# A Fourier mixing layer before a softmax MLP: the step back of the transform on half-size matmul tiles, with the halves joined on VectorE

## Chip, cores and metric

The kernel runs on one core of a Trainium2 chip. The metric is the time of one execution on the device, in microseconds. The kernel before takes 1681.73 us (median of 3 runs, 1681.02 to 1687.88).

## What is computed

Two blocks in sequence, all in float32. First, along the 3136 positions of each of 8 sequences and for each of 256 channels, a real Fourier transform, a product with a complex filter, and the transform back. Then, for each of the 25088 tokens, a layer with 1024 hidden values, their softmax used as a gate, a normalization, and a projection back to 256 values.

```python
X = np.fft.rfft(x, axis=1)                       # x: (8, 3136, 256)
y = np.fft.irfft(X * (filt_r + 1j * filt_i), n=3136, axis=1)
x = y.reshape(25088, 256)
h = x @ w_in                                     # 256 -> 1024
e = np.exp(h - h.max(-1, keepdims=True))
solu = h * e / (e.sum(-1, keepdims=True) + 1e-9)
ln = (solu - solu.mean(-1)) / np.sqrt(solu.var(-1) + 1e-6) * g_ln
return ln @ w_out                                # 1024 -> 256
```

## The kernel before

The transform of length 3136 = 49 x 64 is done in three parts. The **first step** is a transform over 49 (products `pa`). The **spectrum** is a transform over 64, forward (`pb`), the product with the filter on VectorE, and inverse (`pc`). The **step back** over 49 (`py`) writes the sequence into the buffer `y`, channels on the partitions, from which the hidden layer takes its tokens. Intermediate rows go through DRAM. The step back of a sequence is eight pieces; a piece loads 100 rows of 4 KB and makes 4 of the 32 mirrored column pairs:

```python
    def fetch_back(e, ch, rows_pool, split=None):
        split = split or whole
        if rows_pool is not None:
            t4s[e, ch] = rows_pool.tile([P, NCH, C], FP32, ..., tag="r")[0:NK]
        split((nc.sync.dma_start if split is by_16 else nc.gpsimd.dma_start, nc.sync.dma_start),
              t4s[e, ch], d2[e].rearrange("s (a n) c -> (s a) n c", a=4)[:, NCH*ch:NCH*ch+NCH, :])

    def back(e, ch, cb, evac):                   # cb: half of the channels
        ps = ps_t.tile([P, 512], FP32, name=f"py_{e}_{ch}_{cb}", tag="t")
        psv = ps[:, 0:NCH * NR].rearrange("p (m r) -> p m r", r=N1)
        for i in range(NCH):                     # 100 rows deep, 128 wide, 98 columns
            nc.tensor.matmul(out=psv[:, i:2*NCH-i:2*NCH-1-2*i, :],
                             lhsT=t4s[e, ch][:, i, cb*P:cb*P+P], rhs=wi_t, start=True, stop=True)
        ...
        evac(out=y[:, cb, t0:t0+S].rearrange("p (r m j) -> p m j r", ...)[...],
             in_=psv.rearrange("p (m j) r -> p m j r", m=2))
```

Both matrix products of the MLP use Strassen's scheme, seven products of half size where eight would be needed, on **pairs** of token tiles: 256 tokens, 98 pairs in all. `product(j, m)` is one of the seven hidden products of pair j (512 columns each; m in 1, 2, 6, 7, 5, 3, 4 is their order in time), `project(p, m)` one of the seven of the projection (four matmuls of 128 columns each; order 5, 3, 4 in the even step, 1, 2, 6, 7 in the odd one), which belongs to a pair of some steps before. What several products share is kept by a copy on ScalarE (`keep`, `keep_out`) and completed on VectorE (`finish`, `finish_out`):

```python
    def product(j, m):
        bank = {1: 0, 6: 0, 5: 0, 3: 0, 2: 1, 7: 2, 4: 2}[m]
        if m in (1, 2, 7):
            ms[j, bank] = (ps_t.tile(..., tag="t") if m == 2 else ps_m.tile(..., tag=f"m{bank}"))
        ...
        nc.tensor.matmul(out=ms[j, bank], lhsT=lhsT, rhs=w_in_sb[:, w, :],
                         start=m in (1, 2, 7), stop=True, skip_group_check=True)

    def finish_out(p, i, n, kept, bank):
        ot, rs = out_half(p, i, n)
        if kept is None:
            nc.vector.tensor_scalar(out=ot, in0=pos[p, bank], scalar1=rs, ..., op0=ALU.mult)       # L809
        else:
            nc.vector.scalar_tensor_tensor(out=ot, in0=pos[p, bank], scalar=rs,                    # L811
                                           in1=out_half(p, *kept)[0], op0=ALU.mult, op1=ALU.add)
```

The program is a list of steps, two for a pair, and its order on each engine is the order of the text. `early` and `late` hold the transform's jobs of a step: the two halves of a piece of the step back (`cb` 0 early, 1 late), the spectrum's forward products (early), its first multiplication (late) and, in the following odd step, its second multiplication and its inverse products. The parts that matter here, shortened:

```python
    def step(k):
        j, odd = divmod(k, 2)
        ...
        for job in stores[k]: job()                       # odd: difference() of the first step, on VectorE
        if not odd:
            product(j, 1); keep(j, k, 0)
            project(p, 5); keep_out(p, 1, (0, 1))
            product(j, 2)
        else:
            product(j, 5); keep(j, k - 1, 1)
        turn(k - 3)                                       # 32x32 transposes on VectorE
        if not odd:
            finish_out(p, 1, 1, (0, 1), 1); finish(j, k, 0, (k, 0), 1)
        else:
            finish(j, k, 1, (k - 1, 1), 2)
        for job in products[k]: job()                     # second multiplication of the spectrum
        exponential(k - 2)
        for job in early[k]: job()
        if not odd:
            product(j, 6); keep(j, k + 1, 0)
            project(p, 3); project(p, 4)
            ...
            product(j, 7)
        else:
            project(p, 1); keep_out(p, 0, (0, 0)); project(p, 2); finish_out(p, 0, 0, (0, 0), 1)
            product(j, 3); product(j, 4)
            ...
            project(p, 6); project(p, 7)
        normalize(k - 2)
        if not odd:
            finish_out(p, 0, 1, None, 0); finish_out(p, 1, 0, (1, 0), 1); store_out(p)
        else:
            finish(j, k - 1, 1, None, 0); finish(j, k, 0, (k, 0), 2)
            keep_out(p, 1, (1, 0))
        for job in late[k] + loads[k]: job()
```

Which steps hold which jobs is a fixed table. For the sequences 2 to 7 the pieces of the step back stand in even steps, spectrum units start in even steps, and pieces of the first step stand in odd ones; a pair may hold one of each, two of them, one or none. The PSUM pools are `ps_t` (two banks), `ps_b` (two, spectrum), `ps_m` (two, hidden) and `ps_o` (two, projection).

Of the kernel before, what the change touches and what calls it, by code (L numbers as in the profile page):

```python
# [17 lines left out]
P = 128  # L18
# [31 lines left out]
def dft_tables():  # L50
# [19 lines left out]
    for a, part, sign in ((0, 0, 1), (1, 1, -1), (2, 1, 1), (3, 0, 1)):  # L70
# [16 lines left out]
    wq[:, :N1, :, :NK // 2] = wf[1].reshape(N1, NS, 2, 2).transpose(0, 3, 1, 2).reshape(N1, 2, NK // 2)  # L87
    return wf.reshape(NR, NK).astype(f32), wq.reshape(P, 2, 64).astype(f32), \
        wi.reshape(NK, NR).astype(f32), de.astype(f32)
# [3 lines left out]
def kernel(  # L93
# [11 lines left out]
    wf_host, wq_host, wi_host, de_host = dft_tables()  # L105
    wf_dram = nc.inline_tensor(wf_host, name="wf_tbl").ap()
    wq_dram = nc.inline_tensor(wq_host, name="wq_tbl").ap()
    wi_dram = nc.inline_tensor(wi_host, name="wi_tbl").ap()
    de_dram = nc.inline_tensor(de_host, name="de_tbl").ap()
# [16 lines left out]
    wi_t = consts.tile([NK, NR], FP32, name="wi_t")  # L126

# [210 lines left out]
    def fetch_back(e, ch, rows_pool, split=None):  # L338

        split = split or whole  # L340
        if rows_pool is not None:
            t4s[e, ch] = rows_pool.tile([P, NCH, C], FP32, name=f"t4_{e}_{ch}", tag="r")[0:NK]
        split(
            (nc.sync.dma_start if split is by_16 else nc.gpsimd.dma_start, nc.sync.dma_start), t4s[e, ch],
            d2[e].rearrange("s (a n) c -> (s a) n c", a=4)[:, NCH * ch:NCH * ch + NCH, :])
# [14 lines left out]
    with ExitStack() as st:  # L360
# [163 lines left out]
        for i in range(units):  # L524
# [8 lines left out]
            if i == 0:  # L533
                nc.gpsimd.dma_start(out=wi_t, in_=wi_dram)
                nc.gpsimd.dma_start(out=wq_t, in_=wq_dram)
                nc.gpsimd.dma_start(out=g_sb, in_=moe_g_ln.rearrange("(k p) -> p k", p=P))
            elif i != 2:
                begin({1: 2, 3: 3, 4: 4, 5: 5, 6: 6}[i])
# [4 lines left out]
        for ch in range(pieces):  # L543
            fetch_back(0, ch, None, by_16)
# [126 lines left out]
    def product(j, m):  # L671

        bank = {1: 0, 6: 0, 5: 0, 3: 0, 2: 1, 7: 2, 4: 2}[m]
        if m in (1, 2, 7):
            ms[j, bank] = (ps_t.tile([P, DFF // 2], FP32, name=f"m{m}_{j}", tag="t") if m == 2 else
                           ps_m.tile([P, DFF // 2], FP32, name=f"m{m}_{j}", tag=f"m{bank}"))
# [129 lines left out]
    def finish_out(p, i, n, kept, bank):  # L806
        ot, rs = out_half(p, i, n)
        if kept is None:
            nc.vector.tensor_scalar(out=ot, in0=pos[p, bank], scalar1=rs, scalar2=None, op0=ALU.mult)  # L809
        else:  # L810
            nc.vector.scalar_tensor_tensor(out=ot, in0=pos[p, bank], scalar=rs,  # L811
                                           in1=out_half(p, *kept)[0], op0=ALU.mult, op1=ALU.add)
# [204 lines left out]
```

## Time and profile before

| what | value |
|---|---|
| time | 1681.73 us |
| span of the profiled execution | 1680.2 us |
| mean granted clock of TensorE | 0.988 |
| HBM read and written | 124.83 MB and 81.50 MB |
| mean rate of the DMA engines | 186 GB/s |
| loads of the step back, `t<-d` by GpSimd | 56 of 400.0 KB, 4.9 us to landing |

The profile's page is one execution on the chip. A line of its groups reads: source line, engine, operation, output<-inputs by the program's names, shapes, count, then the busy time of the group, the mean of one in ns, and the idle time of the engine just before, with what ended it. PE is TensorE's matmul, PEld its weight load, DVE is VectorE, ACT ScalarE, POOL GpSimd. A float32 matmul appears as two passes, so 512 matmuls of `py` count as 1024. Matmuls are pipelined, and the end of one is modelled: the distance between two starts says what one really costs. A line of the timeline has the start in us, the length in us, then the same names and the count of instructions that are merged; a bracket gives idle time and what ended it. Source lines meant here: L353 is the matmul of the step back and L356 its copy, L680 the hidden products, L792 the projection's, L260 and L292 the first step's and the spectrum's, L313 to L315 the multiplication with the filter, L245 the difference of the first step, L738 `turn`, L704 and L701 `finish`, L723 to L728 `normalize`, L809 and L811 `finish_out`.

### The profile page before, as it was taken

Reading aid. Unit: us, or ns where it says so; the run is one execution under the profiler, and the core shown is the slowest. Engines: PE = TensorE matmul, PEld = TensorE weight load, DVE = VectorE, ACT = ScalarE, POOL = GpSimd, SP = SyncE. Lnnn points to the kernel's source line nnn. Section 1 sums busy time; section 2 is a strip of 40 time slices with the busy share of each in tenths; the row PEclk is TensorE's granted clock in tenths of the full one; section 3 lists DMA queues with packets and bytes.
Section 4 is the critical chain, followed back from the end, with each engine's and each line's share of the span. In section 5 each row is a group of like instructions: output and inputs, shape, how many; then the busy total and the mean of one; then the engine's idle time right before and its main releaser. Section 6 shows DMA issues by size and latency. Waiting matters only on the chain.

```text
span 1680.2 us, 31072 instructions
## 1 busy us (share of the span) xinstructions
PE 1597.7 (95%) x10022; PEld 1094.7 (65%) x10022; DVE 1260.4 (75%) x2619; ACT 939.3 (56%) x1730; POOL 1120.8 (67%) x1268
## 2 busy tenths in 40 slices
PE   5798899999999999999999999999999999999996
PEld 1353356766766676667766676667776777777776
DVE  1676887788777877886878777887778767787773
ACT  2154455656655565566655656556565566655551
POOL 4444786577676766697577866687576766676674
PEclk8999999999999999999999999999999999999999
DMA  9886868786787668865786667766775444444443
GB/s 264 254 278 202 255 180 243 196 220 182 191 224 222 178 182 236 228 182 150 210 243 195 176 166 220 229 181 161 204 213 161 117 125 123 103 106 105 109 112 95
DMA packets 375957, 311.72 MB, mean 186 GB/s; under 512 B 61514, under 2 KB 341571, under 8 KB 375795
## 3 DMA queue, kind: packets, MB, share of 16 engines
q1 hardware_dynamic: 306260, 169.81, 38.5%
q0 software_dynamic: 32640, 101.65, 20.5%
q10 hardware_dynamic: 36896, 38.28, 8.2%
q8 instruction: 81, 1.33, 0.3%
q14 instruction: 80, 0.66, 0.1%
HBM read 124.83 MB, written 81.50 MB: 123 GB/s over the span
## 4 chain that ended last, share of the span: by engine, by line
PE 64%; DMA 17%; DVE 8%; POOL 3%; issue 3%; SPq 2%; ACT 1%; ACTq 0%; DVEq 0%; POOLq 0%
PE m L680 26%; PE o L792 25%; DMA solu_t<-turn 7%; PE py L353 5%; DMA x<-in_x_dram 2%; DMA t<-d 2%; PE pa L260 2%; PE pb L292 2%; PE pc L292 2%; SPq L750 2%; DVE h L728 2%; DVE turn L738 1%; DMA out_dram<-ot 1%; PE pa L217 1%; DVE diff L245 1%
## 5 line engine op out<-in xcount | busy, mean ns | idle before, releaser
L730 ACT ACTIVATE e<-h,nmu 128x1024 f32<-128x1024 f32 x196 | 225.3, 1149 | 360.3 <-DVE h L728 358.8
L792 PEld LDWEIGHTS o<-w_out_sb,solu_t 128*128 128x128 f32 x3136 | 380.3, 192 | 57.8 <-issue 40.7
L792 PE MATMUL o<-w_out_sb,solu_t 128*128 128x128 f32 x3136 | 400.5, 276 | 9.1 <-DVE rsum L723 6.3
L680 PE MATMUL m<-w_in_sb,s 128*128 128x512 f32 x784 | 401.8, 604 | 4.6 <-ACT h L690 2.5
L792 PEld LDWEIGHTS o<-w_out_sb,u 128*128 128x128 f32 x2352 | 305.2, 191 | 147.4 <-issue 113.8
L658 POOL TENSOR_TENSOR u<-solu_t 128x512 f32<-128x512 f32 x98 | 145.3, 1483 | 311.0 <-DMA solu_t<-turn 179.0
L680 PE MATMUL m<-w_in_sb,y 128*128 128x512 f32 x588 | 313.8, 617 | 15.9 <-DVE nmax L704 12.8
L792 PE MATMUL o<-w_out_sb,u 128*128 128x128 f32 x2352 | 312.3, 276 | 7.0 <-ACT ot L804 6.3
L728 DVE SCALAR_TENSOR_TENSOR h<-e,rsum,h 128x1024 f32<-128x1024 f32 x196 | 289.1, 1475 | 6.9
L811 DVE SCALAR_TENSOR_TENSOR ot<-o,rs_t,ot 128x128 f32<-128x128 f32 x294 | 102.5, 349 | 206.6 <-ACT ot L804 170.3
L690 ACT COPY h<-m 128x512 f32<-128x512 f32 x294 | 173.5, 590 | 130.8 <-PE m L680 116.2
L738 DVE STREAM_TRANSPOSE turn<-h 128x1024 f32<-128x1024 f32 x196 | 242.3, 1236 | 0.8
L712 ACT ACTIVATE e<-h,nmax 128x1024 f32<-128x1024 f32 x196 | 226.1, 1154 | 0.0
L658 POOL TENSOR_TENSOR u<-solu_t,u 128x512 f32<-128x512 f32 x98 | 142.7, 1456 | 87.2 <-PE o L792 83.3
L704 DVE CUSTOM_DVE_ANT_0 h<-m,h 128x512 f32<-128x512 f32 x196 | 133.2, 679 | 82.2 <-ACT h L690 59.3
L680 PEld LDWEIGHTS m<-w_in_sb,y 128*128 128x128 f32 x588 | 95.1, 192 | 124.5 <-DVE nmax L704 67.9
L356 ACT COPY y<-py 128x392 f32<-128x392 f32 x128 | 109.6, 856 | 105.4 <-PE py L353 103.8
L353 PEld LDWEIGHTS py<-wi_t,t 100*128 100x128 f32 x1024 | 132.3, 192 | 53.9 <-issue 40.4
L680 PEld LDWEIGHTS m<-w_in_sb,s 128*128 128x128 f32 x784 | 124.0, 191 | 65.9 <-issue 45.7
L658 POOL TENSOR_TENSOR solu_t<-solu_t,solu_t 128x512 f32<-128x512 f32 x98 | 150.8, 1538 | 7.7
L658 POOL TENSOR_TENSOR u<-u,solu_t 128x512 f32<-128x512 f32 x98 | 136.9, 1397 | 0.7
L353 PE MATMUL py<-wi_t,t 100*128 100x98 f32 x1024 | 131.6, 273 | 0.7 <-DMA t<-d 0.4
(108 smaller groups left out, 1978.3 us busy)
## 6 DMA issues: line engine op xcount, KB each, us to landing
solu_t<-turn SPq DMA_DIRECT2D x784, 128.0 KB
out_dram<-ot SPq DMA_DIRECT2D x196, 128.0 KB
t<-d POOLq DMA_DIRECT2D x56, 400.0 KB, 4.9
d<-x POOLq DMA_DIRECT2D x100, 200.0 KB, 5.3
f<-f_dram POOLq DMA_DIRECT2D x39, 512.0 KB, 6.9
d<-g POOLq DMA_DIRECT2D x39, 512.0 KB, 5.1
t<-d ACTq DMA_DIRECT2D x36, 512.0 KB
x<-in_x_dram SPq DMA_DIRECT2D x112, 98.0 KB
```

What stands on the lines that cost most here:

```text
L353: nc.tensor.matmul(out=psv[:, i:2 * NCH - i:2 * NCH - 1 - 2 * i, :], lhsT=t4s[e, ch][:, i, cb * P:cb * P + P], rhs=wi_t, start=True, stop= ...
L356: evac(out=y[:, cb, t0:t0 + S].rearrange("p (r m j) -> p m j r", m=N2 // NCH, j=NCH)[:, ch:last + 1 - ch:last - 2 * ch], in_=psv.rearrange ...
L658: nc.gpsimd.tensor_tensor(out=out, in0=in0, in1=in1, op=op)
L680: nc.tensor.matmul(out=ms[j, bank], lhsT=lhsT, rhs=w_in_sb[:, w, :], start=m in (1, 2, 7), stop=True, skip_group_check=True)
L690: nc.scalar.copy(out=h_half(k, i), in_=ms[j, 0])
L704: nc.vector.tensor_tensor_reduce(out=h_half(k, i), in0=ms[j, bank], in1=h_half(*kept), scale=1.0, scalar=sofar, op0=ALU.add, op1=ALU.min, ...
L712: nc.scalar.activation(out=e, in_=hs[k], func=AFT.Exp, bias=nmaxs.pop(k)[:, 1:2], scale=-1.0, accum_out=esum)
L728: nc.vector.scalar_tensor_tensor(out=solu, in0=e, scalar=rsum, in1=solu, op0=ALU.mult, op1=ALU.mult, accum_out=nmu)
L730: nc.scalar.activation(out=e, in_=solu, func=AFT.Square, bias=nmu, scale=-float(DFF), accum_out=variances[g][:, i:i + 1])
L738: nc.vector.transpose(out=turns[g][:, :, i, :], in_=solus.pop(k).rearrange("p (f j) -> p f j", j=32))
L792: nc.tensor.matmul(out=pos[p, bank], lhsT=lhs[:, f, :], rhs=w[:, f, :], start=f == 0 and m in (1, 2, 7), stop=True, skip_group_check=True)
L811: nc.vector.scalar_tensor_tensor(out=ot, in0=pos[p, bank], scalar=rs, in1=out_half(p, *kept)[0], op0=ALU.mult, op1=ALU.add)
```

## The change

The product over 100 rows is split by the parity of its terms. The even and the odd terms are 50 rows each, and the two outputs of a mirrored pair of columns are their sum and their difference. So a piece needs half the multiplications: 50 rows by 49 columns for each parity, where 100 rows by 98 columns stood. On TensorE this is 32 small matmuls on four 64x64 tiles: the parity chooses the half of the rows, the channel quarter the half of the columns. ScalarE copies the even sums out of PSUM, and VectorE writes sum and difference into `y`. The rows of each parity go to partitions 0 to 49 and 64 to 113, in two loads.

Both halves of the channels are done at once, in one job, with one PSUM bank for each parity, so both banks of `ps_t` are in use. The hidden product 2 leaves `ps_t` for the bank of product 7, and `finish_out` without a kept part moves from VectorE to ScalarE, right after projection product 3. The pieces of batch 0, ahead of the loop, stay as they are.

The core of the diff (tables, names and the batch-0 loads cut):

```diff
+    wb = np.zeros((2, 64, N1))
+    wb[:, :NK // 2] = wi[:, :, 0].reshape(NS, 2, 2, N1).transpose(2, 0, 1, 3).reshape(2, NK // 2, N1)
...
+    def fetch_back(e, ch):
+        t4s[e, ch] = t4 = pools["r"].tile([P, NCH, C], FP32, name=f"t4_{e}_{ch}", tag="r")
+        rows = d2[e].rearrange("s (b j n) c -> j (s b) n c", b=2, j=2)
+        for j in range(2):
+            nc.gpsimd.dma_start(out=t4[64 * j:64 * j + NK // 2],
+                                in_=rows[j, :, NCH * ch:NCH * ch + NCH, :])
+
+    def back_halves(e, ch, pss):
+        t4 = t4s.pop((e, ch))
+        views = [ps.rearrange("p a c -> p (a c)")[:, 0:KD * NCH * N1].rearrange(
+            "p (c i r) -> p c i r", c=KD, i=NCH) for ps in pss]
+        for cb in range(KD):
+            for i in range(NCH):
+                for g in range(2):
+                    rows = slice(64 * g, 64 * g + NK // 2)
+                    for h in range(2):
+                        c0 = cb * P + 64 * h
+                        nc.tensor.matmul(out=views[g][64 * h:64 * h + 64, cb, i, :],
+                                         lhsT=t4[rows, i, c0:c0 + 64], rhs=wb_t[rows],
+                                         start=True, stop=True)
+        even = t4.rearrange("p i c -> p (i c)")[:, 0:KD * NCH * N1]
+        nc.scalar.copy(out=even, in_=pss[0].rearrange("p a c -> p (a c)")[:, 0:KD * NCH * N1])
+        joins[e, ch] = even.rearrange("p (c i r) -> p c i r", c=KD, i=NCH), views[1]
+
+    def join_halves(e, ch):
+        even, odd = (v.rearrange("p c i r -> p c r i") for v in joins.pop((e, ch)))
+        t0, last = e % 2 * S, N2 // NCH - 1
+        to = y[:, :, t0:t0 + S].rearrange("p c (r m j) -> p m c r j", m=N2 // NCH, j=NCH)
+        nc.vector.tensor_tensor(out=to[:, ch], in0=even, in1=odd, op=ALU.add)
+        nc.vector.tensor_tensor(out=to[:, last - ch], in0=even[:, :, :, ::-1], in1=odd[:, :, :, ::-1],
+                                op=ALU.subtract)
...
-            ms[j, bank] = (ps_t.tile([P, DFF // 2], FP32, name=f"m{m}_{j}", tag="t") if m == 2 else
-                           ps_m.tile([P, DFF // 2], FP32, name=f"m{m}_{j}", tag=f"m{bank}"))
+            ms[j, bank] = ps_m.tile([P, DFF // 2], FP32, name=f"m{m}_{j}", tag=f"m{min(bank, 1)}")
...
-            for cb in range(KD):
-                (early, late)[cb][t].append(
-                    lambda e=e, ch=ch, cb=cb: back(e, ch, cb, nc.scalar.copy))
+            (late if ch and t == back_at[ch - 1] else early)[t].append(lambda e=e, ch=ch: back_halves(
+                e, ch, [psum(f"py_{e}_{ch}_{g}") for g in range(2)]))
+            late[t].append(lambda e=e, ch=ch: join_halves(e, ch))
...
                 project(p, 3)
+                keep_out(p, 0, (0, 1))
                 project(p, 4)
...
-                finish_out(p, 0, 1, None, 0)
                 finish_out(p, 1, 0, (1, 0), 1)
```

## The prediction, made before the changed kernel ran

> **What bounds the kernel now.** I read the page from the top: engine totals first, then the groups of the step back (L353, L356), then the timeline of TensorE and of VectorE over single pairs of steps.
>
> ```profile
> PE 1597.7 (95%) x10022; PEld 1094.7 (65%) x10022; DVE 1260.4 (75%) x2619; ACT 939.3 (56%) x1730; POOL 1120.8 (67%) x1268
> L353 PEld LDWEIGHTS py<-wi_t,t 100*128 100x128 f32 x1024 | 132.3, 192 | 53.9 <-issue 40.4
> L356 ACT COPY y<-py 128x392 f32<-128x392 f32 x128 | 109.6, 856 | 105.4 <-PE py L353 103.8
> L353 PE MATMUL py<-wi_t,t 100*128 100x98 f32 x1024 | 131.6, 273 | 0.7 <-DMA t<-d 0.4
> ```
>
> TensorE looks like the bound (95% against 75% on VectorE), and the step back holds 131.6 us of it. A share over the whole span hides that the pairs differ, so I took the start of the first hidden product of each pair from TensorE's timeline. A pair with nothing beside it takes 12.26 us. A pair with one piece of the step back takes 14.15 us (median of 17). Piece and spectrum unit: 16.6 us (12 pairs). Piece, spectrum unit and a piece of the first step: 18.16 us (16 pairs). Piece and first step: 15.25 us (4 pairs). The first batch's three pairs with two or three pieces take 18.3 to 20.2 us. That is 49 + 7 = 56 pieces; the eight of batch 0, ahead of the loop, do not change.
>
> Now one crowded pair **without** the step back (starts 889.53, ends 906.66: 17.13 us), then one **with** it (871.54 to 889.53: 17.99 us), TensorE's timeline from the pair's middle on:
>
> ```profile
> 896.13 1.88 PE L680 MATMUL m<-w_in_sb,s 128*128 128x512 f32 x4
> 897.85 1.95 PE L792 MATMUL o<-w_out_sb,solu_t 128*128 128x128 f32 x16
> 899.64 1.02 PE L680 MATMUL m<-w_in_sb,s 128*128 128x512 f32 x2
> 901.48 1.13 PE L680 MATMUL m<-w_in_sb,y 128*128 128x512 f32 x2 [0.82 <-DVE nmax L704]
> ...
> 903.67 1.16 PE L792 MATMUL o<-w_out_sb,solu_t 128*128 128x128 f32 x8 [0.17 <-DVE rsum L723]
> ```
>
> ```profile
> 879.00 1.02 PE L680 MATMUL m<-w_in_sb,s 128*128 128x512 f32 x2
> 879.87 1.03 PE L353 MATMUL py<-wi_t,t 100*128 100x98 f32 x8
> 880.73 1.05 PE L680 MATMUL m<-w_in_sb,s 128*128 128x512 f32 x2
> ...
> 886.54 1.16 PE L792 MATMUL o<-w_out_sb,solu_t 128*128 128x128 f32 x8 [0.17 <-DVE rsum L723]
> ```
>
> The piece is two products of 0.87 us each (early and late), yet the pair grows by only 0.86 us: the late one (879.87) fills the time in which the other pair waits 0.82 us for VectorE. So crowded pairs are held by VectorE. Its timeline in the same pair has no idle time from the last output half of the even step to the one that frees the projection's bank:
>
> ```profile
> 879.21 0.35 DVE L811 SCALAR_TENSOR_TENSOR ot<-o,rs_t,ot 128x128 f32<-128x128 f32 x1 [0.54 <-PE o L792]
> 879.48 0.68 DVE L313 TENSOR_TENSOR pr<-pb,f 128x512 f32<-128x512 f32 x1
> ...
> 882.48 1.23 DVE L738 STREAM_TRANSPOSE turn<-h 128x1024 f32<-128x1024 f32 x1
> 883.64 0.65 DVE L704 CUSTOM_DVE_ANT_0 h<-m,h 128x512 f32<-128x512 f32 x1
> ...
> 886.14 0.34 DVE L811 SCALAR_TENSOR_TENSOR ot<-o,rs_t,ot 128x128 f32<-128x128 f32 x1
> ```
>
> The loop of such a pair: TensorE's fourth projection product ends (879.2), VectorE works 7.3 us through, TensorE's seventh projection product may start (886.54), and TensorE then runs 10.6 us unbroken to the next fourth product. In a pair with a piece alone VectorE has room; at the same place it sat idle 1.58 us for the kept half:
>
> ```profile
> 1373.28 0.69 DVE L704 CUSTOM_DVE_ANT_0 h<-m,h 128x512 f32<-128x512 f32 x1 [1.58 <-ACT h L690]
> ```
>
> [...] 16 loads of 133 ns of the spectrum lie within 0.66 us in the timeline, and the py group ahead of a tiled group takes 0.96 us to the next start (874.25 to 875.21) instead of 0.86. [...] the py groups run at 0.87/8 = 109 ns[...]. [...] The copy L356, which writes single values 256 bytes apart, agrees: 856 ns for 392 values, where copies of 256 and 512 values in line take 361 and 590 ns (482 by interpolation).
>
> **The change part by part.**
> - *TensorE.* Out: two groups of 0.87 us a piece, 1.74 us. In: 32 products on four tiles, 64 passes, 16 rounds of four. [...] half of 109 plus some, say 58 ns: 16 x 58 = 0.93 us. If no spectrum unit stands next to it, a second mode change of some 0.10 us at each side: 1.1 us. So TensorE sheds 0.65 us in a pair with a piece alone, 0.8 us in a crowded one: 56 pieces, about 40 us of work.
> - *Where it lies.* All of it now stands early, in the place of the first half (0.87 + a mode change, so about equal). What goes is the late half, and in crowded pairs that stood in a wait.
> - *VectorE.* In: two joins of 392 values a piece. L314 takes 678 ns for 512 values and 405 ns for 256, from its two shapes in the groups, so 550 ns for 392; two with the 0.08 us by which neighbours overlap are 0.95 us. Both inputs are read 196 bytes apart; if that costs what L356 pays, another 0.4 us each: 1.75 us. I take J = 1.25 us. They stand after the L811 of the even step and ahead of the spectrum's multiplication, that is, inside the unbroken 7.3 us. Out: L809, 98 x 348 ns = 34 us; but it runs while VectorE waits 0.54 us for the next product, so nothing of it is on the loop.
> - *ScalarE.* Out: 112 copies of 856 ns; in: 56 of 482 ns and 98 scaled copies of 363 ns: 33 us less, off the path (56% busy).
> - *Transfers and bank.* One load of 400 KB becomes two of 200 KB, with 0.6 us more of GpSimd's issue each; loads are sent one to three steps ahead and land in 4.9 us: hidden. The second hidden product now waits until L704 has read the bank of the pair before; in the pair above that ended at 889.41, and the second product started at 891.39, 2.0 us later. Nothing.
>
> **The sum, by pairs.** Three parts and crowded: J in full, 16 x 1.25 = +20 us. Piece and spectrum: there the seventh projection product started 0.3 us after VectorE was done, so 12 x 0.95 = +11.4 us. Piece alone: -0.65 to -0.7, 17 x 0.7 = -12 us (the 1.58 us of idle time less the 0.87 us that TensorE comes earlier, plus the slack after it, still hold J). Piece and first step: 4 x 0.7 = -3 us. First batch: two or three late halves of 0.87 us go and only J stands against them, about -1 us in each of three pairs. Together +13 us: 1695 us.
>
> **Rivals.** (a) *TensorE is the bound and its gain goes through.* For it: 95%, and 64% of the chain that ended last. Against it: the 0.82 us wait above that the late half fills. It would give 1682 - 40 = 1642 us. (b) *The joins are cheap or dear.* With J = 0.95: 16 x 0.95 + 12 x 0.65 - 18 = +5, 1687 us. With J = 1.75: 28 + 17, and the lone pieces keep only 0.4 us of their gain, -9: 1718 us. (c) *Small tiled products are paced by issue, not by loads.* No group before has so many: 128 instructions of weights and products in 0.93 us, where the spectrum's densest has 32 in 0.86 us. At the spectrum's pace of 54 ns a product it would be 64 x 54 = 3.5 us, far above 1.74; at half of that 1.7 us, and some 0.8 us more for each of 49 pairs, 1735 us. The overlapping loads speak against it. (d) *A new wait on the shared bank or on the two transfers*: slack of one to two us in the pairs read, so little.
>
> **Range and chances.** My middle is J = 1.25. The cheap join and a little luck in waits give the low side, the dear join or a slowed stream the high side: 1668 to 1725 us. Faster by over 2% (below 1648) needs (a): 0.10. Slower by over 2% (above 1715) needs the dear join or (c): 0.28. The rest 0.62.
>
> **What would show it.** The new product group's time to the next start: 0.9 to 1.1 us (right), 1.7 and up (c). The joins' mean: 550 ns (cheap), 900 or more (dear). Crowded pairs grown by about J, with longer waits of the m<-y product on nmax and of the o<-solu_t product on rsum; lone pieces 13.4 us instead of 14.15; plain pairs still 12.3 us. I am wrong if crowded pairs shrink too: then VectorE's chain had slack that I did not see, or the joins left it.

## The result, and the profile after

The changed kernel takes 1732.92 us (median of 4 runs, 1726.11 to 1735.69) where the kernel before takes 1682.43 us beside it: a ratio of 1.0283, with an interval of 1.0255 to 1.0311. Ratios are to runs of the kernel before on the same chip, and later kernels are compared by them. The change is slower, and it lies above the range of the prediction, which ended at 1725 us.

The engine totals of the page of after:

```profile
PE 1584.7 (92%) x12710; PEld 1057.9 (61%) x12710; DVE 1291.6 (75%) x2633; ACT 906.2 (52%) x1772; POOL 1121.5 (65%) x1325
```

TensorE's share fell from 95% to 92% because the span grew while its work shrank by 13 us. Its work was not what set the time. The groups of the new step back (after, kept apart by shape; L367 is the small matmul, L371 the copy, L379 and L380 the joins):

```profile
L367 PE MATMUL py<-wb_t,t 50*64 50x49 f32 x3584 | 65.7, 220 | 1.6 <-issue 1.6
...
L379 DVE TENSOR_TENSOR y<-t,py 128x392 f32<-128x392 f32 x56 | 46.0, 821 | 1.7 <-ACT t L371 1.7
L380 DVE TENSOR_TENSOR y<-t,py 128x392 f32<-128x392 f32 x56 | 45.6, 815 | 0.0
...
L371 ACT COPY t<-py 128x392 f32<-128x392 f32 x56 | 27.1, 485 | 21.9 <-PE py L367 21.7
```

The L353 of before (131.6 us) also holds the eight pieces of batch 0, some 16 us, which do not change; so the matmuls of the other 56 pieces went from about 115 us to 65.7 us. One block of them takes 0.97 us from its first start to the next product's (480.50 to 481.47), within the 0.93 to 1.1 us of the prediction. The copy is 485 ns, as interpolated. The joins are 820 ns each and not 550 ns.

Now a crowded pair with all three parts, 888.61 to 908.10 us: 19.49 us, where the pair of the prediction took 17.99 us. First TensorE's timeline from the pair's middle on, then VectorE's (L716 is now the hidden product, L828 the projection, L844 `finish_out`, L740 `finish`, L759 and L764 `normalize`, L317 to L319 the filter, L249 the difference of the first step, L774 `turn`):

```profile
899.67 1.02 PE L716 MATMUL m<-w_in_sb,s 128*128 128x512 f32 x2
902.92 1.12 PE L716 MATMUL m<-w_in_sb,y 128*128 128x512 f32 x2 [2.22 <-DVE nmax L740]
903.88 1.05 PE L828 MATMUL o<-w_out_sb,u 128*128 128x128 f32 x8
905.10 1.16 PE L828 MATMUL o<-w_out_sb,solu_t 128*128 128x128 f32 x8 [0.17 <-DVE rsum L759]
```

```profile
896.37 0.35 DVE L844 SCALAR_TENSOR_TENSOR ot<-o,rs_t,ot 128x128 f32<-128x128 f32 x1 [2.10 <-PE o L828]
896.64 0.82 DVE L379 TENSOR_TENSOR y<-t,py 128x392 f32<-128x392 f32 x1
897.38 0.81 DVE L380 TENSOR_TENSOR y<-t,py 128x392 f32<-128x392 f32 x1
898.12 0.67 DVE L317 TENSOR_TENSOR pr<-pb,f 128x512 f32<-128x512 f32 x1
...
904.70 0.35 DVE L844 SCALAR_TENSOR_TENSOR ot<-o,rs_t,ot 128x128 f32<-128x128 f32 x1
```

The joins stand where the prediction put them, inside VectorE's unbroken work. From 896.37 to the end of the last L844 it is 8.68 us, where the same stretch before was 7.27 us. The starts from the first join on are 0.74 us apart twice, so the two joins hold VectorE 1.48 us, which is about the growth of 1.41 us. TensorE stands 2.22 us for `nmax`.

The waits, summed over the span (engine, line, releaser: us in total, times, longest), of after and then of before:

```profile
POOL u L695 <- DMA solu_t<-turn: 277.7, 76, 8.1
PEld m L716 <- DVE nmax L740: 124.5, 96, 3.9
PE m L716 <- DVE nmax L740: 59.3, 39, 3.1
DVE diff L249 <- DMA x<-in_x_dram: 12.8, 6, 5.7
```

```profile
POOL u L658 <- DMA solu_t<-turn: 179.0, 47, 7.9
PEld m L680 <- DVE nmax L704: 68.1, 83, 3.7
PE m L680 <- DVE nmax L704: 12.8, 16, 2.9
```

TensorE's wait for `nmax` grew by 46.5 us: that is VectorE's chain. But two lines have nothing to do with joins: GpSimd, which makes the sums `u` for the projection, waits 99 us longer for the transfer `solu_t<-turn`, and the first step's difference waits for its rows `x`, which it did not before. `solu_t<-turn` brings the transposed blocks to their partitions, from one buffer on the chip to another. It runs on the first DMA queue, whose line (packets, MB, share of 16 engines) reads before and after:

```profile
q1 hardware_dynamic: 306260, 169.81, 38.5%
```

```profile
q1 hardware_dynamic: 306260, 169.81, 46.8%
```

The packets and bytes are equal, and the time in them is longer. The trace's packet records give it to the 200,704 packets of 512 bytes, which are `solu_t<-turn`: 43.5 ns each on average after, 31.9 ns before. The prediction had nothing on this.

Pair periods, as in the prediction (from the first hidden product of a pair to that of the next, medians in us), with the kernels of the experiments that the account rests on:

| pair (count) | before | after | e1 | e5 | e12 | e10 |
|---|---|---|---|---|---|---|
| piece alone (17) | 14.15 | 13.54 | 13.54 | 13.54 | 13.54 | 13.54 |
| piece, first step (4) | 15.25 | 14.91 | 14.74 | 14.90 | 14.74 | 14.74 |
| piece, spectrum (12) | 16.62 | 17.81 | 16.42 | 17.80 | 17.29 | 16.34 |
| all three (16) | 18.16 | 20.51 | 19.15 | 19.12 | 18.87 | 18.12 |
| first step alone (11) | 13.63 | 14.38 | 14.84 | 13.52 | 13.52 | 13.52 |

### The profile page after: what moved, and what is told of

Its sections match the earlier page's. It is cut to its first block, busy times and chain, and to the rows that moved or that the text cites. A ratio compares the mean times of both kernels' runs of the same rounds, so it can differ in the third digit from the quotient of the medians.

```text
span 1728.4 us, 36835 instructions
## 1 busy us (share of the span) xinstructions
PE 1584.7 (92%) x12710; PEld 1057.9 (61%) x12710; DVE 1291.6 (75%) x2633; ACT 906.2 (52%) x1772; POOL 1121.5 (65%) x1325
## 4 chain that ended last, share of the span: by engine, by line
PE 58%; DMA 21%; DVE 9%; SPq 3%; issue 3%; POOL 3%; ACT 1%; ACTq 0%; DVEq 0%; POOLq 0%
PE o L828 24%; PE m L716 24%; DMA solu_t<-turn 9%; PE py L367 3%; DMA x<-in_x_dram 2%; SPq L786 2%; DMA de<-de_tbl 2%; PE pb L296 2%; PE pa L264 2%; DVE turn L774 2%; DMA out_dram<-ot 2%; DVE h L764 2%; DMA t<-d 1%; PE pc L296 1%; DMA d<-x 1%
## 5 line engine op out<-in xcount | busy, mean ns | idle before, releaser
L828 PEld LDWEIGHTS o<-w_out_sb,solu_t 128*128 128x128 f32 x3136 | 385.2, 194 | 58.9 <-issue 38.0
L828 PE MATMUL o<-w_out_sb,solu_t 128*128 128x128 f32 x3136 | 405.6, 278 | 9.0 <-DVE rsum L759 5.9
L716 PE MATMUL m<-w_in_sb,s 128*128 128x512 f32 x784 | 396.3, 607 | 12.6 <-ACT h L726 11.3
L828 PEld LDWEIGHTS o<-w_out_sb,u 128*128 128x128 f32 x2352 | 313.6, 196 | 150.9 <-issue 114.1
L695 POOL TENSOR_TENSOR u<-solu_t 128x512 f32<-128x512 f32 x98 | 138.6, 1414 | 391.4 <-DMA solu_t<-turn 277.7
L716 PE MATMUL m<-w_in_sb,y 128*128 128x512 f32 x588 | 318.4, 625 | 61.4 <-DVE nmax L740 59.3
L828 PE MATMUL o<-w_out_sb,u 128*128 128x128 f32 x2352 | 319.4, 280 | 9.7 <-ACT ot L840 9.7
L844 DVE SCALAR_TENSOR_TENSOR ot<-o,rs_t,ot 128x128 f32<-128x128 f32 x294 | 102.6, 349 | 282.7 <-ACT ot L840 163.4
L764 DVE SCALAR_TENSOR_TENSOR h<-e,rsum,h 128x1024 f32<-128x1024 f32 x196 | 280.7, 1432 | 6.9
L774 DVE STREAM_TRANSPOSE turn<-h 128x1024 f32<-128x1024 f32 x196 | 242.6, 1238 | 0.5
L716 PEld LDWEIGHTS m<-w_in_sb,y 128*128 128x128 f32 x588 | 94.2, 193 | 175.3 <-DVE nmax L740 124.5
L716 PEld LDWEIGHTS m<-w_in_sb,s 128*128 128x128 f32 x784 | 128.7, 192 | 100.1 <-issue 80.5
L840 ACT ACTIVATE ot<-o,rs_t 128x128 f32<-128x128 f32 x392 | 142.4, 363 | 72.5 <-PE o L828 65.7
L740 DVE CUSTOM_DVE_ANT_0 h<-m,h 128x512 f32<-128x512 f32 x196 | 132.1, 674 | 42.2 <-ACT h L726 25.7
L695 POOL TENSOR_TENSOR solu_t<-solu_t,solu_t 128x512 f32<-128x512 f32 x98 | 130.3, 1329 | 7.7
L695 POOL TENSOR_TENSOR s<-y 128x128 f32<-128x128 f32 x196 | 105.4, 538 | 1.6 <-DVE y L380 0.7
L367 PEld LDWEIGHTS py<-wb_t,t 50*64 50x64 f32 x3584 | 58.3, 134 | 44.5 <-PE o L828 14.4
```

The costliest lines, as they stand in the source:

```text
L367: nc.tensor.matmul(out=views[g][64 * h:64 * h + 64, cb, i, :], lhsT=t4[rows, i, c0:c0 + 64], rhs=wb_t[rows], start=True, stop=True)
L695: nc.gpsimd.tensor_tensor(out=out, in0=in0, in1=in1, op=op)
L740: nc.vector.tensor_tensor_reduce(out=h_half(k, i), in0=ms[j, bank], in1=h_half(*kept), scale=1.0, scalar=sofar, op0=ALU.add, op1=ALU.min, ...
L764: nc.vector.scalar_tensor_tensor(out=solu, in0=e, scalar=rsum, in1=solu, op0=ALU.mult, op1=ALU.mult, accum_out=nmu)
L774: nc.vector.transpose(out=turns[g][:, :, i, :], in_=solus.pop(k).rearrange("p (f j) -> p f j", j=32))
L828: nc.tensor.matmul(out=pos[p, bank], lhsT=lhs[:, f, :], rhs=w[:, f, :], start=f == 0 and m in (1, 2, 7), stop=True, skip_group_check=True)
```

## Experiments: joins, bank and clock

My theory after the result was the prediction's own, VectorE's chain lengthened by dear joins. The rivals were the two transfers of 50 rows, the shared bank, and something in the clock of TensorE.

**e1: joins of the even steps ahead of the last `finish_out`.** There VectorE waits for TensorE in any case (2.10 us at 896.37 above).

```diff
-            late[t].append(lambda e=e, ch=ch: join_halves(e, ch))
+            (late if t % 2 or ch and t == back_at[ch - 1] else joined)[t].append(
+                lambda e=e, ch=ch: join_halves(e, ch))
...
+        for job in joined[k]:                       # after normalize(k - 2)
+            job()
         if not odd:
             if proj:
                 finish_out(p, 1, 0, (1, 0), 1)
```

> The changed kernel with one thing moved: in even steps the two joins stand right after normalize, ahead of the last output half (L844 in the changed kernel), where VectorE waits 2.1 to 2.5 us for TensorE's fourth projection product in the crowded pairs. Theory (the joins lengthen VectorE's unbroken chain between the fourth and the seventh projection product): crowded pairs with all three parts fall from 20.5 us to about 18.0, pairs of piece and spectrum unit from 17.8 to about 16.4, lone pieces stay at 13.54; 16 x 2.3 + 12 x 1.4 = 54 us less, about 1679 us. Rival (the tiled products themselves, or the shared bank, or the two loads cost the time): the pairs stay where they are, 1725 to 1735 us.

Measured: 1708.73 us, ratio 1.0169 (1.0137 to 1.0201). Pairs of piece and spectrum fell as the theory says, to 16.42 us. Pairs with all three stopped at 19.15 us, not 18.0, and the first step's pairs rose to 14.84. So the place of the joins is one cause, and something else remains; GpSimd's wait for `solu_t` stayed at 279.1 us.

**e2: the sum written a second time.**

```diff
         nc.vector.tensor_tensor(out=to[:, ch], in0=even, in1=odd, op=ALU.add)
+        nc.vector.tensor_tensor(out=to[:, ch], in0=even, in1=odd, op=ALU.add)
```

> The changed kernel with the first join (the sum) written twice, same place, same result: one more VectorE instruction of 0.82 us a piece, 0.74 us between starts. Theory (VectorE's chain is on the path in crowded pairs, off it in lone ones): 28 crowded pairs grow by 0.74 us each, lone pieces by 0 to 0.3, together 20 to 25 us more, about 1755 us. Rival (TensorE or waits elsewhere set the pairs): under 5 us more.

Measured: 1781.75 us, ratio 1.06 (1.0538 to 1.0662): 49 us more for 56 instructions. Pairs of piece and spectrum rose by 1.87 us for 0.74 us of work. The direction confirms VectorE's chain. The size is over twice what was expected. Lone pieces rose by 0.53 us (13.54 to 14.07), where 0 to 0.3 was expected, and TensorE's granted clock was at half for 121 us after the first 120 us of the span, against 61 us in after and 25 us in before.

**e3: the bank and the moved `finish_out` alone, in the kernel before.**

```diff
+            ms[j, bank] = ps_m.tile([P, DFF // 2], FP32, name=f"m{m}_{j}", tag=f"m{min(bank, 1)}")
...
                 project(p, 3)
+                keep_out(p, 0, (0, 1))
...
-                finish_out(p, 0, 1, None, 0)
```

> The kernel before with only the second part of the change: hidden product 2 in the bank of product 7, and the first output half without a kept part scaled on ScalarE right after projection product 3 and no longer on VectorE. The step back is the old one. Prediction's claim: nothing, 1682 us within 4, pairs unchanged. Rival (product 2 or 7 now waits for VectorE's reading of the shared bank): 0.2 us or more in each of 98 pairs, 1700 us and above.

Measured: 1686.07 us, ratio 1.0013 (0.9997 to 1.0029). This part costs nothing, as predicted.

**e4: TensorE kept busy in its wait,** by two products that nobody reads, between the hidden products 3 and 4 of 15 crowded pairs.

```diff
                 product(j, 3)
+                fill(k)       # two 512-column matmuls into a bank of ps_t
                 product(j, 4)
```

> The changed kernel with two matmuls of 512 columns whose result nobody reads, put between hidden products 3 and 4 in the 15 pairs of sequences 2 to 7 that hold all three parts, where TensorE waits 2.1 us for VectorE. They add work in the wait. Theory (the wait of over 2 us lets the granted clock fall to a half for 3.4 us, which costs 1.3 us in every pair where it happens): the low-clock stretches in those pairs go away, the pairs at 20.5 to 20.8 us fall to 19.1 to 19.4, about 10 us less in all, 1722 us. Rival (the 20.5 us have another cause, and the low clock comes with it): no change, or up to 0.3 us more a pair.

Measured: 1727.78 us, ratio 1.0279. The crowded pairs fell from 20.51 to 19.47 us in the median, and the time at half clock from 61 to 35 us, so the clock drop is real; the sum over them fell by 5 us only, and the ratio did not move beyond its error. In after's timeline, such a drop:

```profile
491.87 1.12 PE L716 MATMUL m<-w_in_sb,y 128*128 128x512 f32 x2 [2.08 <-DVE nmax L740]
492.83 1.76 PE L828 MATMUL o<-w_out_sb,u 128*128 128x128 f32 x8
494.38 1.92 PE L828 MATMUL o<-w_out_sb,solu_t 128*128 128x128 f32 x8
```

After 2.08 us of waiting, eight instructions that took 1.05 us in the pair above take 1.76. The granted clock is 0.5 there for 3.4 us: of the 14 stretches at 0.5 that after has behind its first 120 us, 12 are 3.4 us long. A wait of over 2 us often has one beside it: 11 of the 15 such waits that L716 had in after stand beside a stretch at half clock, four do not.

## Experiments: where the tiles lie

A tile is here a buffer in the chip's memory, as the program allocates it, and its start is counted in bytes within a partition. The new table `wb_t` has 49 columns of 4 bytes and takes 224 bytes of each partition. It stands ahead of nearly everything else, so the change moves all tiles behind it. In the program as built, `turn` and `solu_t` start 256 bytes past a multiple of 512 in the kernel before, and 480 past one after the change.

**e5: the change with `wb_t` in 64 columns.** Then both start on a multiple of 512.

```diff
-    wb_t = consts.tile([P, N1], FP32, name="wb_t")
+    wb_t = consts.tile([P, 64], FP32, name="wb_t")[:, 0:N1]
```

> The changed kernel whole, with the new table wb_t in a tile of 64 columns (256 bytes) instead of 49 (196, which take 224). In the two kernels as built the tiles behind the tables (y, h, turn, solu_t, x, t) start at multiples of 64 bytes before the change and 32 bytes past one after it; this edit puts them back on multiples of 64. In the traces the 512-byte packets of the transfer solu_t<-turn took 44 ns each after the change and 32 ns before it, 200704 of them. Theory 'alignment': the packets return to 32 ns, the first queue's share to about 38.5% (from 46.8%), GpSimd's waits for solu_t to about 180 us (from 278), A pairs to about 13.6 us (from 14.4), pairs with all three parts to about 19.5 us or less (from 20.5), the time to 1700-1715 us (after: 1733). Rival 'two transfers': the 50-row loads crowd the queue; then nothing changes, 1733 us, 44 ns.

Measured: 1709.65 us, ratio 1.0134 (1.0102 to 1.0166), from 1.0283. Fifteen columns of padding are worth 1.5%, some 25 us. The 512-byte packets are back at 32.8 ns, GpSimd's wait for `solu_t` at 125.9 us, the first step's pairs at 13.52 us. The queue's line:

```profile
q1 hardware_dynamic: 306260, 169.81, 38.4%
```

The two transfers of 50 rows are still in it. They cost nothing visible.

**e6: the kernel before, moved by 32 bytes.**

```diff
-    wi_t = consts.tile([NK, NR], FP32, name="wi_t")
+    wi_t = consts.tile([NK, NR + 8], FP32, name="wi_t")[:, 0:NR]
```

> The kernel before with nothing but its tables' end moved: wi_t in a tile of 106 columns instead of 98 (32 bytes more), of which 98 are used, so that all tiles behind it start 32 bytes past a multiple of 64, as in the changed kernel. Alignment: packets of solu_t<-turn 44 ns, the first queue near 46%, GpSimd's waits for solu_t near 280 us, and some 5 to 25 us more than before (1688-1708). If the two transfers or the joins make the packets slow: 32 ns and the time of before, 1682.

Measured: 1730.19 us, ratio 1.0255 (1.0214 to 1.0295). No operation differs from the kernel before, and it is as slow as the changed one. The loss is more than I expected, with packets of 36.7 ns only.

**e7: e1 with `wb_t` in 64 columns.**

> e1 (joins of the even steps ahead of the last finish_out) with wb_t in 64 columns. Alignment: pairs with all three parts fall from 19.15 (e1) to about 18.2 us, A pairs to 13.6, the sum over e1's 1709 about 25 us less: 1675-1690. If the crowded pairs of e1 were held by the collisions of VectorE and GpSimd alone: pairs with all three parts stay at 19.15, time 1700 or more.

Measured: 1670.61 us, ratio 0.99 (0.9867 to 0.9934): faster than the kernel before. Pairs with all three 18.11 us. What was left over in e1 was the tiles' place; the collisions of VectorE and GpSimd were not it.

**e8: the old step back where a spectrum unit stands, the new one elsewhere,** `wb_t` in 64 columns.

```diff
+                t, t - 1, spectrum_at[-1] + 2,
+                lambda e=e, ch=ch, f=fetch_whole if t in crowded else fetch_back: f(e, ch)))
+            if t in crowded:
+                for cb in range(KD):
+                    (early, late)[cb][t].append(
+                        lambda e=e, ch=ch, cb=cb: back(e, ch, cb, nc.scalar.copy))
+                continue
```

> Old step back (one load of 100 rows, signs in the table, ScalarE's scattered copy) for pieces in pairs with a spectrum unit, the new one (two loads, joins on VectorE) for the 17 lone pieces and the 4 pairs with a first step alone; bank and keep_out of the change; wb_t in 64 columns. If the loss sits in the crowded pairs' VectorE chain and in the alignment: those pairs at before's 18.1 and 16.6 us, lone pieces at 13.5, so before minus 17 x 0.61 and 4 x 0.35: 1670 us (1664-1678), faster than both. If the two transfers or the start cost something of their own: 1682 or more.

Measured: 1674.88 us, ratio 0.9934 (0.9906 to 0.9962). Crowded pairs are at 18.19 and 16.52 us, lone pieces at 13.64 us. As expected, and not better than e7.

## Experiments: the disputed costs by themselves

**e9: transfers and joins alone.** The kernel computes nothing of the reference and stores zeros.

```diff
+    for s0, d0 in CASES: moves(s0, d0)              # 16 transfers of 128 KB each, as solu_t<-turn
+    for n in range(12): nc.vector.tensor_tensor(out=to[:, n], in0=e, in1=o, op=ALU.add)   # and five more forms
```

> The disputed costs by themselves; nothing of the reference is computed, the output is zeros. First the transfer of solu_t<-turn (16 transfers of 128 KB, packets of 512 bytes) between two tiles that start on multiples of 512 bytes, nine times, with source and destination moved by (0,0), (32,0), (0,32), (32,32), (64,64), (480,480), (288,288), (256,256), (0,0) bytes. Then the two joins of the step back twelve times each: operands and order as in the change (sum, difference), with both operands stored so that they are read in line (sum, difference), read in line and written in single values (sum), and all in line. Alignment: packets of 32 ns at (0,0), (64,64), (256,256), 36-44 ns wherever 32 bytes past a multiple of 64, the more the whole path; a rival, that the move in the kernels changes who meets whom and not the packet, gives 32 ns everywhere. Joins: if the strided read (values 196 bytes apart) makes the 820 ns, the in-line forms take about 500-550; if PSUM or four-value runs do, they stay near 800.

The joins, by line (L54, L57 sum and difference as in the change; L60, L63 with operands stored so that they are read in line; L66 read in line, written in single values; L69 all in line):

```profile
L54 DVE TENSOR_TENSOR y<-ev,od 128x392 f32<-128x392 f32 x12 | 8.7, 800 | 0.0
L57 DVE TENSOR_TENSOR y<-ev,od 128x392 f32<-128x392 f32 x12 | 8.7, 788 | 0.0
L66 DVE TENSOR_TENSOR y<-ev,od 128x392 f32<-128x392 f32 x12 | 8.1, 831 | 0.0
L69 DVE TENSOR_TENSOR flat<-ev,od 128x392 f32<-128x392 f32 x12 | 6.8, 563 | 0.4
L60 DVE TENSOR_TENSOR y<-ev,od 128x392 f32<-128x392 f32 x12 | 5.9, 546 | 0.0
L63 DVE TENSOR_TENSOR y<-ev,od 128x392 f32<-128x392 f32 x12 | 5.8, 556 | 0.0
```

Reading in line takes 550 ns, reading 196 bytes apart 800, writing single values 256 bytes apart 831. Writing runs of four values costs nothing (546 against 563 with all in line), and since all six forms read one operand from PSUM, PSUM does not make the difference. So the 550 of the prediction was right for operands in line, and the stride is the 250 ns. Of the transfers, the first three cases ran beside the store of the zeros, which took 72 to 74% of the DMA engines' time in each: 30.8 ns at (0, 0), 36.1 with the source 32 bytes on, 30.7 with the destination 32 bytes on. The fourth, (32, 32), met only the end of that store and took 34.6; the last five had 35.3 ns at 64 bytes, 43.1 at 480, 33.5 at 288, 31.5 at 256 and 31.9 at 0.

**e10: e7 with the four columns of a piece side by side in PSUM,** so that ScalarE copies in line and the joins read in line.

```diff
-            "p (c i r) -> p c i r", c=KD, i=NCH) for ps in pss]
+            "p (c r i) -> p c i r", c=KD, i=NCH) for ps in pss]
...
-        joins[e, ch] = even.rearrange("p (c i r) -> p c i r", c=KD, i=NCH), views[1]
+        joins[e, ch] = even.rearrange("p (c r i) -> p c i r", c=KD, i=NCH), views[1]
```

> e7 (joins early, wb_t in 64 columns) with the products of the step back written into their banks with the four columns of a piece side by side (out in steps of 16 bytes), so that ScalarE copies in line and the joins read in line. If the strided read is what made the joins dear: 550 ns each instead of 820, pairs with all three parts about 0.2 to 0.5 us less, 1660-1670 us (e7: 1671). If TensorE's strided write costs: the block 0.97 us grows and the lone pieces rise over 13.54; time 1671 or more.

Measured: 1668.33 us, ratio 0.9906 (0.9891 to 0.992). This is the fastest version, 0.9% below the kernel before; against e7 the intervals overlap. TensorE's writes in steps of 16 bytes cost nothing: lone pieces stay at 13.54 us, and L367's busy time is 64.6 us. The joins in it:

```profile
L379 DVE TENSOR_TENSOR y<-t,py 128x392 f32<-128x392 f32 x56 | 31.1, 555 | 2.1 <-ACT t L371 2.1
L380 DVE TENSOR_TENSOR y<-t,py 128x392 f32<-128x392 f32 x56 | 30.9, 553 | 0.0
```

Crowded pairs hardly moved (18.12 us, where 0.2 to 0.5 us less than e7's 18.11 was expected): once the joins stand in a wait, their length matters little.

**e11: the transfer alone again,** with a wait between the cases.

> The transfer of solu_t<-turn alone again, without other transfers beside it and with a wait between the cases; nothing of the reference is computed, the output is zeros. Twelve cases of 4096 packets of 512 bytes; source and destination start (0,0), (32,32), (64,64), (128,128), (256,256), (288,288), (448,448), (480,480), (480,0), (0,480), (0,0), (480,480) bytes past a multiple of 512. In e9, where the first cases met other transfers, the last ones took 35 ns at 64, 43 at 480, 33.5 at 288, 31.5 at 256 and 32 at 0. If the start within 512 bytes matters: about 32 ns at 0 and 256, 33 to 35 at 32, 64, 128 and 288, 43 at 480 (the tiles of the changed kernel), and the pair of (480,0) and (0,480) says whether source or destination pays. If e9's differences came from what ran beside: 32 ns in all.

The stores of zeros again ran beside the first three cases, so the nine behind them count. Mean of 4096 packets of 512 bytes, by the start of source and destination past a multiple of 512 bytes:

| source, destination | ns |
|---|---|
| 0, 0 and 256, 256 | 32.0 |
| 288, 288 | 34.1 |
| 128, 128 | 35.5 |
| 448, 448 | 42.2 |
| 480, 480 (twice) | 43.9, 43.4 |
| 480, 0 | 43.7 |
| 0, 480 | 32.3 |

Here the source pays and the destination does not. The queue's line in the two last cases of the table, (480, 0) and then (0, 480), each over 11.7 us (173.9 to 185.6, then 185.6 to 197.3), shows it too: nearly the same packets, 96.5% against 72.2%.

```profile
q1 hardware_dynamic: 4336, 2.09, 96.5%
```

```profile
q1 hardware_dynamic: 4367, 2.10, 72.2%
```

With the source 0, 32, 128, 192 and 224 bytes past a multiple of 256, the packet takes 32.0, 34.1, 35.5, 42.2 and 43.4 to 43.9 ns. What makes it so is not shown.

**e12: e5 with the joins reading in line, at the change's place.** This is the prediction's cheap case: joins of 0.55 us each, and transfers as before.

> The changed kernel with wb_t in 64 columns (as e5) and the products of the step back written side by side (as e10), the joins left where the change puts them. What the prediction assumed, then: joins of 0.55 us each and transfers as before. If its sum was right but for the dear joins and the place of the tiles: e5's 1710 less 28 crowded pairs x 0.53 us = 15, that is 1695 us (1690-1700), pairs with all three parts near 18.6 to 19.0 us, pairs without a first step near 17.3. If the joins' length matters less than their place: 1700 or more.

Measured: 1691.34 us, ratio 1.0032 (1.002 to 1.0044). TensorE's wait for `nmax` in e12, then in e10, where the joins stand early:

```profile
PE m L716 <- DVE nmax L740: 46.2, 41, 2.5
```

```profile
PE m L716 <- DVE nmax L740: 20.3, 28, 1.6
```

## Experiments: which tiles

**e13, e14: the source alone put back.** The source `turn` is moved within a longer tile, in the changed kernel (e13) and in e6 (e14, with 56 in place of 8), to a multiple of 512; all other tiles stay where they were.

```diff
-            turns[g] = wk2.tile([P, DFF // 32, 4, 32], FP32, name=f"turn_{g}", tag="turn")
+            room = wk2.tile([P, 4 * DFF + 128], FP32, name=f"turn_{g}", tag="turn")
+            turns[g] = room[:, 8:8 + 4 * DFF].rearrange("p (f k j) -> p f k j", k=4, j=32)
```

> The changed kernel as it stands, wb_t in 49 columns, and all tiles 32 bytes past a multiple of 64, but for one: turn, the source of solu_t<-turn, is moved 32 bytes on in a longer tile, to a multiple of 512. If the start of that source is the whole of the part that the place of the tiles has in the loss: packets 32-33 ns and e5's time, 1.013 times before (1708). If the other tiles, written by transfers from HBM, pay as well: between 1.016 and 1.028 (1714-1733).

Measured: 1723.79 us, ratio 1.0233 (1.0217 to 1.0248).

> e6 (the kernel before with all tiles 32 bytes further on) with turn alone put back on a multiple of 512. The source alone: packets 32 ns and the time of before, ratio 1.00. Others pay: ratio 1.01 or more; e6's packets were only 36.7 ns against 44 after the change, yet its ratio was 1.0255, so this run may well stay above 1.

Measured: 1717.76 us, ratio 1.0189 (1.0167 to 1.021). In both the source gives back a part only, and the rest lies in other tiles.

**e15: the source alone moved, in the kernel before,** by the same edit with 56.

> The kernel before with turn alone moved to 480 bytes past a multiple of 512 (where the change puts it), all other tiles on the offsets that they have before. Packets 43-45 ns. If the source alone costs what the change lost by its tiles' place: ratio 1.01 to 1.02 (1700-1720). If it is the other tiles: ratio near 1.00 with slow packets.

Measured: 1688.02 us, ratio 1.0021 (1.0007 to 1.0036). The packets took 40.7 ns, and GpSimd waited as long as in the changed kernel:

```profile
POOL u L658 <- DMA solu_t<-turn: 268.0, 70, 7.9
```

And yet it costs 0.2%. My reading of that wait, and of the slow packets, as the loss itself was wrong: the sums `u` had room.

**e16, e17, e18: groups of tiles moved in the kernel before,** by gaps of 8 columns between the pools: the tiles of the spectrum and of the rows (e16), `solu_t` with `h`, `e` and the sums (e17, where the rows behind them move on by 64 bytes in all), the weights and `y` (e18, where the tiles behind move on by 64 bytes in all).

```diff
+    pool("gap0", 1).tile([P, 8], FP32, name="gap0")
     upool = pool("up", 2)
```

> The kernel before with a gap of 32 bytes ahead of the tiles of the spectrum steps alone (the rows x and t loaded from HBM, the products and g that are stored there, the tables de), so that these start 32 bytes past a multiple of 64; turn, solu_t, h, y and the weights stay. If these tiles make e14's 1.9%: ratio 1.015 to 1.02, packets of 1024 bytes 56 ns instead of 53.5. If not: 1.00.

> The kernel before with solu_t, h, e and the sums u and s alone moved to 32 bytes past a multiple of 64 (a gap of 32 bytes ahead of them and another behind). If the destination of solu_t<-turn pays when other transfers run beside it, or VectorE, ScalarE and GpSimd pay for such operands: ratio 1.005 to 1.02, packets of 512 bytes 34-35 ns. If not: 1.00.

> The kernel before with the weights, y and the small tiles alone 32 bytes past a multiple of 64 (a second gap behind them puts the others on multiples of 64). No transfer of the main loop reads or writes them but the rows of deviations, so: ratio 1.00; if TensorE's weight loads from y or the engines' reads pay: more than 1.005.

Measured: 1693.7, 1710.26 and 1713.8 us, ratios 1.005 (1.0031 to 1.0069), 1.0142 (1.0097 to 1.0188) and 1.0171 (1.0122 to 1.0221). Beside all others (starts in bytes past a multiple of 512, packets of 512 bytes; for after and e13 the ratio is divided by e5's 1.0134):

| kernel | `turn` | `solu_t` | packet, ns | ratio |
|---|---|---|---|---|
| before | 256 | 256 | 31.9 | 1 |
| e16 | 256 | 256 | 32.4 | 1.005 |
| e15 | 480 | 256 | 40.7 | 1.002 |
| e17 | 256 | 288 | 34.5 | 1.014 |
| e18 | 320 | 320 | 36.5 | 1.017 |
| e14 | 0 | 288 | 34.8 | 1.019 |
| e6 | 288 | 288 | 36.7 | 1.026 |
| e13 | 0 | 480 | 35.8 | 1.010 |
| after | 480 | 480 | 43.5 | 1.015 |

Every kernel of the table with `solu_t` off a multiple of 256 loses 1.0 to 2.6%, and none with it on one loses more than 0.5%. My expectations spoke of multiples of 64; e18 has its tiles on those, and loses. The engines' own instructions do not explain it. ScalarE's copies (L690 in before) take 590 ns in before, 591 in e17 and 589 in e6, the transposes (L738) 1236, 1236 and 1237; and where VectorE's means vary, they do not follow the loss (L728: 1475 ns in before, 1499 in e16, 1480 in e6, which lost most). Nor did the destination cost anything with a free queue (e11: 32.3 ns at 480 against 32.0) or beside stores of zeros (e9: 30.7 ns at 32 against 30.8), so if it pays in the kernel, it pays beside other transfers than those: in e17 the middle packet is 32 ns as before, and the slowest tenth starts at 47 ns where it was 38. That `solu_t` is the tile of its group which counts is an inference, since it is the only one there that a transfer touches. It was not moved alone: `h`, `e` and the sums moved with it each time, and e17 and e18 also put the rows on 320. So it is shown that the place of the tiles costs this time, and that the source `turn` is the smaller part; that the destination is the larger one is not shown, nor why.

## Why the prediction was wrong

Step by step:

- **Crowded pairs are held by VectorE's chain.** Right. With the joins taken out of it the pairs are back at the periods of before (e7, and e10 against e12), and a third addition lengthens them (e2). Rival (a), TensorE as the bound, falls with this: its work shrank in every pair with a piece, and those with all three parts still take 18.12 us in e10, where it was 18.16.
- **The block of 0.93 to 1.1 us, lone pieces at 13.4 us, plain pairs unchanged.** Right: 0.97 us where a spectrum unit follows and 1.08 us where a hidden product does (31 and 21 blocks of after), 13.54 us, and 12.26 to 12.42 us in both kernels. The 58 ns a round was an estimate from the 109 ns of before; what sets the pace of a block is not shown. The pairs with a first step beside the piece gained 0.34 us, where 0.7 was said. Rival (c), pacing by issue at 54 or 27 ns a product, falls: 64 passes in 0.97 us are 15 ns each. Whether both parities could write one PSUM bank is not tested by any run.
- **Bank, L809, two transfers: nothing.** Right for the bank and L809 (e3). The two transfers were not tried alone; e5 and e12 have them, and the small matmuls (L367) wait for no transfer there.
- **J = 1.25 us.** Mis-sized. The joins are nearly the dear ones of rival (b), 0.82 us each; J is 1.48 us from start to start. The text named the stride of 196 bytes as the doubt and then split the difference. Put J = 1.48 into its sum: 16 x 1.48 + 12 x 1.18 - 18 = +20 us. e5, which has these joins and the tiles in good places, is at +23 us. With joins of 0.55 us, the cheap case was 16 x 0.95 + 12 x 0.65 - 18 = +5 us; e12 is at 1691.34 - 1686.33 = +5.0 us. So the sum was right in form, and its term J was off by 0.23 us a pair, 6 us over 28 pairs. Part of this agreement is luck: pairs of piece and spectrum grew as booked (1.18 us in e5, 0.67 in e12), but those with all three, where J was booked in full, grew by 0.96 us and not 1.48 (e5), and by 0.71 and not 0.95 (e12), in the median.
- **Transfers otherwise as before.** This is the step that failed. The new table moves the tiles behind it, and 1.5% (some 25 us) of the 50 come from that. The diff shows a tile of 49 columns and nothing more. That transfers add nothing was argued from the two loads that the diff names, and the transfer that suffered is one that it doesn't touch. This is why the time fell out of the range: 1682 + 20 lies inside it.

The account of the 2.83%: place of the tiles 1.49, strided reading 1.02, late joins in line less what TensorE saves 0.32. By the intervals of the ratios the first is good to some 0.4, the second to some 0.3. The lost clock (e4) is inside these.

## What to carry to other kernels

A new tile ahead of others is a change to all of them: look up the starts in both built programs, and pad a table so that the tiles behind it stay on multiples of 256 bytes, as `turn` and `solu_t` do in the kernel before and in e5 (1709.65 us, where the change took 1732.92). Before a gain on TensorE is booked, ask which engine is handed the work and at which place: here the same joins in line cost 1.3%, 21 us, more inside a chain (e12) than in a wait (e10). And lay out what a product leaves in PSUM for the engine that reads it, since the product's own strided write was free (L367's busy time 64.6 us in e10, 65.7 us in line).

## What the runs showed of the hardware that I had not expected

- 32 bytes: the kernel before, moved by 32 bytes and otherwise unchanged, takes 1730 us and not 1687 (e6).
- A 512-byte packet between tiles takes 32 ns from a source on a multiple of 256 bytes and 44 ns from 32 bytes below one; moving the destination alone changes 0.3 ns (e11).
- A float32 addition of 392 values takes 550 ns with operands in line, 800 with both read 196 bytes apart, 831 written 256 bytes apart (e9).
- Matmuls on 64x64 tiles that write 49 values in steps of 16 bytes into PSUM took as long as in line (64.6 us against 65.7 us in sum, e10).
- A wait of 2.1 us on TensorE can be followed by 3.4 us at half clock; eight matmul passes then took 1.76 us instead of 1.05 (after). Two products that fill such waits brought the time at half clock from 61 to 35 us (e4).
